# Matmuls of one fused kernel cut into 64-row halves, two heads' sums and two side sums open at a time

## The chip, the core and the metric

The kernel runs on one core of one Trainium2 chip. The metric is the device time of a run in microseconds (us). The engines are named as the profile names them: PE (TensorE matmul), PEld (its weight loads), DVE (VectorE), ACT (ScalarE), POOL (GpSimd) and SP (SyncE, which here issues most DMAs).

## The reference

Two independent computations share one kernel; their outputs are put side by side.

```python
# A: a long convolution (S4): a kernel of 2048 taps per channel, 576 channels, applied through an FFT
K = einsum("dn,dnl,dn->dl", Cc, exp(dt*A*l), dt*B).real;  y = irfft(rfft(u)*rfft(K))[:2048] + u*Dskip
# B: attention, 32 query heads of 18 columns, one key head and one value head; S = 2048, D = 576
q = (x @ wq) per head; k = x @ wk; v = x @ wv
p = softmax(q k^T * 18**-0.5);  out = concat_heads(p @ v) @ wo
```

## The kernel before

**Attention.** Queries are worked in four chunks of 512 (`c`), heads in groups of four (`g`, eight per chunk), keys in 16 blocks of 128 (`kb`). One *step* is one (c, g, kb): two *pairs* of heads (`j`), so there are 512 steps and 1024 pairs. For each pair, `scores` (L501) multiplies a key block by the two heads' queries in f16: the two heads' 55 rows lie at rows 0 and 64 of the array, so both matmuls, 64 rows by 128 columns, run at once into the two PSUM banks of one tile `s`. `exponentials` (L512) then makes a tile `P` of 128x1024 on ACT. `product` (L802) multiplies the four heads' `P` by the values in f32, four matmuls of 128 rows by 32 columns side by side, and sums over the 16 key blocks in one PSUM bank, `ops`, which DVE copies out (`gather`).

PSUM has eight banks: three tiles `s` of two banks (`NS = 3`), one bank for `ops`, one (`bank()`, tag `f`) for everything else. The loop in `main` goes in rounds of NS pairs: three scores one after the other, their three exponentials, then products and side work until the tiles `s` are expected to be free.

**Side work on PE**, all in f32 and in 128 rows by 32 columns: query projections `q` (`qproj`, L395) for later chunks, the output projection `op` (`outproj`, `outproj_part`), small bounds `up`, and the convolution's matmuls: its taps `kg` (`kgen`, L1236), its transforms `hu`, `lu`, `hk`, `lk` (`transform`) and `iy` (`back`). DVE does the convolution's elementwise work between them and empties each bank.

**What sets the order.** PE, DVE and ACT are ordered by hand: `main` records instructions in the order in which a planner's clocks (`K.t` for PE, `K.v` for DVE, `K.a` for ACT) say that they become ready. Side work comes from generators (streams) that yield after each piece: kind `"p"` for a piece on PE, `"v"` for one on DVE; a stream that holds the bank `f` goes on before any other may take it. `state["credit"]` rations how much side work goes into a round; `RATE` and `PACE` ration the convolution's DVE work per step. Every engine executes its instructions in the recorded order.

Of the kernel before, what the change touches and what calls it, by code (L numbers as in the profile page):

```python
# [9 lines left out]
F32 = mybir.dt.float32  # L10
# [32 lines left out]
NS = 3  # L43
# [3 lines left out]
RATE = 1.90  # L47
PACE = 1.83
# [5 lines left out]
DEFER = 0.5  # L54
NAUG = 5
# [20 lines left out]
class Clock:  # L76
# [6 lines left out]
    def __init__(self):  # L83
        self.t = self.v = self.a = 0.0
        self.work = 0.0
        self.last = ""
        self.s = [0.0] * NS
        self.fill = 0.0

    def pe(self, cost, *after):  # L90
        self.t = max(self.t, *after) + cost if after else self.t + cost
# [103 lines left out]

class Attention:
# [7 lines left out]
    def __init__(self, tc, ctx, aps, clock):  # L204
# [11 lines left out]
        self.ps_f = pool("ps_f", 1, space=PSUM)  # L216

# [3 lines left out]
    def bank(self, n, name):  # L221
        self.k.pe(0.0, self.k.fill)
        return self.ps_f.tile([P, CT], F32, tag="f", name=name)[:, :n]
# [9 lines left out]
    def setup(self, tp, conv):  # L233
# [24 lines left out]
        nc.gpsimd.memset(x0[64:, 4, :], 0.0)  # L258
        nc.gpsimd.memset(xr[64:, 4], 0.0)
# [27 lines left out]
        p1, small = (self.ps_s.tile([P, 2, CT], F32, tag="s", name=n)[:, 0, :] for n in ("first", "small"))  # L287
        p2 = self.bank(CT, "second")
        pv = self.ps_o.tile([P, CT], F32, tag="o", name="vps")

        def queries(ps, j, k):
            nc.tensor.matmul(ps[32 * j:32 * j + 32, :], self.wq[0][:, k, 32 * j:32 * j + 32], x0[:, k, :],
                             start=(k == 0), stop=(k == 4), tile_position=(0, 32 * j))

        def project(ps, j, i, c, k):
            nc.tensor.matmul(ps[32 * j:32 * j + 32, :], wkv[:, k, i:i + 32], xr[:, k, c - 1, :] if c else x0[:, k, :],
# [51 lines left out]
    def settle(self, conv):  # L348
# [4 lines left out]
        vp = self.bank(CT, "vp").rearrange("p (j n) -> p j n", j=4)  # L353
# [6 lines left out]
        pk = self.bank(20, "kmx")  # L360
# [4 lines left out]
        V.tensor_scalar(self.kmax, self.kmax, FLOOR, 1.002, op0=ALU.max, op1=ALU.mult)  # L365
        for m in range(2, 5):
# [9 lines left out]
    def load_wo(self):  # L376
        self.nc.vector.memset(self.wo[0:1, :, 0:1], 0.0)
        for m, (m0, mn) in enumerate(MT):
            self.nc.sync.dma_start(self.wo[:mn, m, :], self.a["wo"][m0:m0 + mn, :])

    def qproj(self, c, m, xt):

        nc, V, K = self.nc, self.V, self.k
        w, nf = self.wq[m], 2 if m < 4 else 1
        self.q_left = 5 * nf
        yield "p", K.fill, False
        ps = self.bank(CT, f"q{c}_{m}")
        for f in range(nf):
            for k in range(5):
                for j in range(4):  # L390

                    o = slice(32 * j, 32 * j + 32)
                    i = o if m < 4 else slice(32 * (j % 2), 32 * (j % 2) + 32)
                    x = slice(256 * f, 256 * f + 256) if m < 4 else slice(256 * (j // 2), 256 * (j // 2) + 256)
# [1157 lines left out]
```

## Time and profile before

| | us |
|---|---|
| runs (3) | 1164.48 to 1169.69, median 1167.79 |
| the profiled execution: its own time | 1169.43 |
| its span, first to last instruction | 1167.6 |
| PE busy / DVE busy / ACT busy / POOL busy | 1084.9 / 997.3 / 999.3 / 143.3 |
| mean granted TensorE clock | 0.99 |

The profile is one execution. In its rows a group of instructions has a count, its busy time, the mean duration of one in ns, and the idle time ahead of it with what ended it. Matmuls overlap in the array, so a matmul's recorded duration is longer than the distance between two of them; one f32 matmul leaves two records and one f16 matmul leaves one. In a timeline row stand the start, the length of the whole run of equal instructions, and their number.

### The profile page before, as it was taken

To read this page: it belongs to the slowest core of one execution; us is meant where nothing else is said; L and a number is where in the kernel's file an instruction comes from. 1 tells how busy PE (TensorE), PEld (TensorE's weight loads), DVE (VectorE), ACT (ScalarE), POOL (GpSimd) and SP (SyncE) were. 2 spreads that over 40 slices of the span, in tenths; PEclk is the share of its full clock that TensorE was granted. 3 is DMA by queue.
4 is the path that set the end of the run, shared out by engine and by line. 5 is a ranking of instruction groups with operands and counts; after the bars stand their busy time and mean duration, and the time that the engine had idled before them with its cause. 6 is when DMAs were issued, how large, how long until landed. Compare 5 with 4: busy or idle time off the path is not lost.

```text
span 1167.6 us, 33030 instructions
## 1 busy us (share of the span) xinstructions
PE 1084.9 (93%) x13862; PEld 391.0 (33%) x13862; DVE 997.3 (85%) x1741; ACT 999.3 (86%) x1052; POOL 143.3 (12%) x257
## 2 busy tenths in 40 slices
PE   6999899999999999889999999999889999998997
PEld 1333233333333333223333333334323333333233
DVE  3797997998996998998899797998898898897853
ACT  2888979898888988998888898888989988998993
POOL 5421320112022000001122000001220000000000
PEclk9899999999999999999999999999999999999999
DMA  7412242114113102112223202112212202112111
GB/s 224 141 41 75 75 140 79 49 41 136 37 61 104 53 29 86 36 65 85 85 83 97 85 20 71 50 55 79 72 40 76 87 29 74 59 48 69 35 42 44
DMA packets 58750, 83.35 MB, mean 71 GB/s; under 512 B 14467, under 2 KB 34679, under 8 KB 58085
## 3 DMA queue, kind: packets, MB, share of 16 engines
q1 hardware_dynamic: 47173, 73.39, 19.5%
q0 software_dynamic: 10848, 7.37, 2.5%
q8 instruction: 110, 1.80, 0.6%
q10 hardware_dynamic: 576, 0.43, 0.1%
q14 instruction: 43, 0.35, 0.1%
HBM read 46.59 MB, written 33.85 MB: 69 GB/s over the span
## 4 chain that ended last, share of the span: by engine, by line
PE 54%; DVE 25%; ACT 12%; issue 7%; DMA 2%; SPq 0%; ACTq 0%; DVEq 0%
PE ops L802 22%; PE s L501 14%; ACT P L512 11%; DVE tab L119 4%; PE op L193 4%; PE q L395 3%; PE iy L193 3%; PE kg L1236 3%; DVE acc L119 3%; DVE ks L119 3%; DVE pt L119 2%; DVE t L119 2%; DVE fr L119 1%; DMA xr<-xT 1%; PE hk L193 1%
## 5 line engine op out<-in xcount | busy, mean ns | idle before, releaser
L512 ACT ACTIVATE P<-s 128x1024 f32<-128x1024 f32 x992 | 934.8, 1034 | 123.1 <-PE s L501 121.6
L802 PE MATMUL ops<-P,v_sb 128*32 128x512 f32 x4096 | 513.4, 600 | 12.7 <-DVE o L123 12.4
L501 PE MATMUL s<-aug,kaug 55*128 55x512 f16 x2048 | 308.7, 383 | 40.0 <-ACT P L512 36.1
L501 PEld LDWEIGHTS <-kaug 55*128 55x128 f16 x2048 | 90.5, 94 | 374.3 <-issue 330.9
L802 PEld LDWEIGHTS ops<-P,v_sb 128*32 128x32 f32 x4096 | 116.2, 110 | 166.6 <-issue 124.1
L445 POOL DMA_DIRECT2D qd<-qh x116 | 65.8, 574 | 337.5 <-DVE qh L127 334.9
L395 PE MATMUL q<-x,wq_sb 128*32 128x256 f32 x1360 | 84.6, 385 | 3.4 <-DVE sck L119 2.5
L193 PE MATMUL op<-wo_sb,oT 126*32 126x288 f32 (+1 forms) x1104 | 79.6, 411 | 1.1 <-DVE ob L123 1.1
L119 DVE TENSOR_TENSOR tab<-tab,tt 128x576 f32<-128x576 f32 (+1 forms) x72 | 59.2, 823 | 1.6
L119 DVE TENSOR_TENSOR tt<-fr,sum 128x576 f32<-128x576 f32 (+1 forms) x72 | 58.9, 819 | 0.0
L119 DVE TENSOR_TENSOR tab<-tab 128x576 f32<-128x576 f32 (+1 forms) x72 | 58.9, 818 | 0.0
L119 DVE TENSOR_TENSOR tab<-sum,fr 128x576 f32<-128x576 f32 (+1 forms) x72 | 58.9, 818 | 0.0
L119 DVE TENSOR_TENSOR tab<-fr,dif 128x576 f32<-128x576 f32 (+1 forms) x72 | 58.8, 817 | 0.0
L123 DVE COPY ksb<-kg 128x192 f32<-128x192 f32 x48 | 17.4, 362 | 47.6 <-PE kg L1236 47.3
L395 PEld LDWEIGHTS q<-x,wq_sb 128*32 128x32 f32 x1360 | 40.1, 110 | 44.1 <-issue 18.1
L1145 POOL MEMSET fr<- 128x192 f32 x24 | 12.8, 618 | 301.8 <-DVE tt L119 176.3
L119 DVE TENSOR_TENSOR acc<-acc,pt 128x1728 f32<-128x1728 f32 (+2 forms) x36 | 48.7, 1352 | 0.1
L119 DVE TENSOR_TENSOR pt<-us,ks 128x1728 f32<-128x1728 f32 (+2 forms) x36 | 48.4, 1352 | 0.1
L510 ACT ACTIVATE P<-s,bias 128x1024 f32<-128x1024 f32 x32 | 33.2, 1114 | 15.1 <-PE s L501 14.7
L193 PEld LDWEIGHTS op<-wo_sb,oT 126*32 126x32 f32 (+1 forms) x1104 | 30.4, 109 | 42.1 <-issue 17.8
L1236 PE MATMUL kg<-tab 128*32 128x64 f32 x2304 | 41.9, 220 | 2.5 <-DVE tab L119 1.6
L1236 PEld LDWEIGHTS kg<-tab 128*32 128x32 f32 x2304 | 35.5, 110 | 25.2 <-issue 9.2
(157 smaller groups left out, 1023.2 us busy)
## 6 DMA issues: line engine op xcount, KB each, us to landing
od<-o SPq DMA_DIRECT2D x31, 256.0 KB
aug<-qd SPq DMA_DIRECT2D x124, 55.0 KB
u<-u SPq DMA_DIRECT2D x12, 384.0 KB
kd<-ksb SPq DMA_DIRECT2D x12, 384.0 KB
kt<-kd SPq DMA_DIRECT2D x48, 96.0 KB
outa<-u SPq DMA_DIRECT2D x12, 384.0 KB
pw<-pw SPq DMA_DIRECT2D x8, 528.0 KB
oT<-od SPq DMA_DIRECT2D x16, 252.0 KB
```

The lines of the kernel that those rows point to most:

```text
L119: return self.v.tensor_tensor(out, *a, **k)
L123: return self.v.tensor_copy(out, *a, **k)
L193: nc.tensor.matmul(ps[j:e], w[:, j:e], x, start=start, stop=stop, tile_position=(0, j))
L395: nc.tensor.matmul(ps[o, 256 * f:256 * f + 256], w[:, k, i], xt[:, k, x], start=(k == 0), stop=(k == 4), tile_position=(0, 32 * j))
L445: q.dma_start(qd[h:h + n, row + d:row + d + nd, cs], src[i1:i1 + n * nd, :cs.stop - cs.start])
L501: nc.tensor.matmul(ps[:, j, :], self.kaug[r, kb * P:(kb + 1) * P], t[r, :], start=True, stop=True)
L510: nc.scalar.activation(pt, ps, AF.Exp, bias=self.bias, scale=SCALE / QQ)
L512: nc.scalar.activation(pt, ps, AF.Exp, scale=SCALE / QQ)
L802: nc.tensor.matmul(o_ps[32 * j:32 * j + 32, :], self.v[:, kb, :], pts[2 * n + j // 2][:, j % 2, :], start=(kb == 0), stop=(kb == 15), tile ...
L1145: nc.gpsimd.memset(t[:, :, 0:NF:8], one)
L1236: nc.tensor.matmul(ps[32 * g:32 * g + 32, d, :], t[:, :32], t[:, 32:], start=(j == 0), stop=(j == 1), tile_position=(0, 32 * g))
```

## The change

All products of the loop take tiles of 64 rows by 32 columns instead of 128 by 32 (or, for scores, 64 by 128).

- **Two sums at a time.** A new class `Turns` gives `part`: eight matmuls, four on rows 0 to 63 that add to one bank (`y = role`) and four on rows 64 to 127 that add to the other. Then the halves change banks: a second `part` with the other role completes both sums. Its first matmul waits on a semaphore that the last matmul of the first part sets, since the halves swap the banks that they write.
- **Heads.** `schedule()` pairs the last eight key blocks of one group of heads with the first eight of the next; their two sums are the two banks of `ops` (`obank`). A step of four pairs makes two parts. The first eight and the last 24 key blocks stand alone and stay at 128 rows.
- **Side work.** `bank()` gives two banks. `q`, `op`, `up`, `hu`/`lu`/`hk`/`lk` (now one tile `fu`, `fk`) and `iy` are made in the two roles; `kg` stays at 128 rows. Rows 64 to 127 of the fifth tile of x and wq, of which only 64 were in use, now hold a copy of the first 64, so that `q` takes nine parts for its two halves of queries; the fifth tile of `oT` and `wo` is padded with zeros to 100 rows. One DVE copy empties both banks.
- **Scores** become eight matmuls for a pair, 55 rows by 32 columns.
- **PSUM**: two tiles `s` (`NS = 2`, four banks), two banks for `ops`, two for side work. The loop goes pair by pair: `work(i)` places products and side pieces until tile `s` is free, then come one pair's scores. `DUE` and `LIMIT_P` say how many pairs after its exponentials a part may, and must, be placed.
- The planner's numbers are new: 0.12 us when the rows change, `SWAP` 0.36 us between two parts, `RATE` 1.87, `PACE` 1.80, `DEFER` 0.35, `NAUG` 6.

```diff
-NS = 3
+NS = 2
-RATE = 1.90
-PACE = 1.83
+RATE = 1.87
+PACE = 1.80
-    def pe(self, cost, *after):
+    def pe(self, cost, *after, rows=64):
+        if rows != self.rows:
+            self.t += 0.12
+            self.rows = rows
...
+class Turns:
+    def part(self, nc, role, outs, ws, xs, rows=((0, 64), (64, 128)), start=False, stop=False, first=False, last=False, only=None):
+        m = None
+        for r in (0, 1):
+            lo, hi = rows[r]
+            y = r ^ role
+            if hi <= lo or only is not None and y != only:
+                continue
+            for j in range(4):
+                w, x = ws(y, j), xs(y, j)
+                q = nc.tensor.matmul(outs(y, j), w[lo:hi], x[lo:hi], start=start if start in (0, 1) else start[y], stop=stop if stop in (0, 1) else stop[y], tile_position=(64 * r, 32 * j))
+                if m is None and first:
+                    q.wait_op(self.sem, self.n, "sem-ge")
+                m = q
+        if last:
+            self.n += 1
+            m.then_inc(self.sem, 1)
...
     def scores(self, i, c, pr, kb, cost):
-            nc.tensor.matmul(ps[:, j, :], self.kaug[r, kb * P:(kb + 1) * P], t[r, :], start=True, stop=True)
+            for b in range(0, P, 32):
+                nc.tensor.matmul(ps[b:b + 32, j, :], self.kaug[r, kb * P + b:kb * P + b + 32], t[r, :], start=True, stop=True, tile_position=(64 * j, b))
...
-        def product(n):
-            for j in range(4):
-                nc.tensor.matmul(o_ps[32 * j:32 * j + 32, :], self.v[:, kb, :], pts[2 * n + j // 2][:, j % 2, :],
-                                 start=(kb == 0), stop=(kb == 15), tile_position=(0, 32 * j))
+        def product():
+            if len(st) == 2:
+                q = self.to.part(nc, state["role"], lambda y, j: o_ps[y][32 * j:32 * j + 32, :], lambda y, j: self.v[:, at[y][1], :],
+                                 lambda y, j: pts[at[y][0] + j // 2][:, j % 2, :], start=[ph == 0 and at[y][1] == 0 for y in (0, 1)],
+                                 stop=[ph == 1 and at[y][1] == 15 for y in (0, 1)], first=(ph == 1), last=(ph == 0))
+                state["swap"] = K.t + SWAP
...
-        for r in range(0, len(pairs), NS):
-            new = range(r, min(r + NS, len(pairs)))
-            for i in new:
-                ss[i] = self.scores(i, c, 2 * g + j, kb, 0.34 if i == r else 0.216)
+        for i, (c, g, kb, j, n, y) in enumerate(pairs):
+            if i > 2:
+                work(i)
+            ss = self.scores(i, c, 2 * g + j, kb, 0.216)
...
+def schedule():
+    group = lambda n, kb: (n // 8, n % 8, kb, n % 2)
+    steps = [[group(0, kb)] for kb in range(8)]
+    for t in range(8, 8 * (8 * NCH - 1)):
+        n = t // 8
+        steps.append(sorted((group(n, t % 8), group(n - 1, 8 + t % 8)), key=lambda x: x[3]))
+    steps += [[group(8 * NCH - 2, kb)] for kb in range(8, 16)]
+    steps += [[group(8 * NCH - 1, kb)] for kb in range(16)]
```

Where the change moves PE's instructions, two places show it. The first is the loop in the middle of the run, on PE: `s` are scores (the two numbers in a name are the head pair within the chunk and the key block), `ops` are products (the number is the group of heads), `kaug` is a weight load for scores. Before, there are three scores, then products at 128 rows.

```order
L802 MATMUL ops_5_6292<-P_10_9_6429,v_sb 32x512 x2
L802 MATMUL ops_5_6292<-P_11_9_6449,v_sb 32x512 x2
L802 MATMUL ops_5_6292<-P_10_10_6451,v_sb 32x512 x2
L802 MATMUL ops_5_6292<-P_11_10_6453,v_sb 32x512 x2
L501 LDWEIGHTS kaug
L501 MATMUL s_11_12_6493<-aug_112,kaug 128x512 [waits Activation_49]
L501 MATMUL s_10_13_6496<-aug_111,kaug 128x512 [waits Activation_49]
L501 MATMUL s_11_13_6499<-aug_112,kaug 128x512 [waits Activation_49]
L802 MATMUL ops_5_6292<-P_10_11_6474,v_sb 32x512 x2
```

After, on PE in the same part of the loop, one part of a product stands between two pairs' scores, half of it for each of two groups; the second part, with the banks exchanged, comes two pairs later and waits for the semaphore `o`.

```order
L218 MATMUL ops_1_7158<-P_2_9_7986,v_sb 32x512 x2
L218 MATMUL ops_1_7158<-P_3_9_8044,v_sb 32x512 x2
L218 MATMUL ops_2_8025<-P_4_1_7953,v_sb 32x512 x2
L218 MATMUL ops_2_8025<-P_5_1_7964,v_sb 32x512 x2
L565 LDWEIGHTS kaug
L565 MATMUL s_2_10_8100<-aug_110,kaug 32x512 [waits Activation_49]
L565 MATMUL s_3_10_8119<-aug_111,kaug 32x512 [waits Activation_49]
L218 MATMUL ops_2_8025<-P_4_1_7953,v_sb 32x512 [waits o]
L218 MATMUL ops_2_8025<-P_5_1_7964,v_sb 32x512 x2
L218 MATMUL ops_1_7158<-P_2_9_7986,v_sb 32x512 x2
L565 MATMUL s_4_3_8138<-aug_112,kaug 32x512 [waits Activation_49]
```

So the order on PE goes from threes of scores with 128-row work between to single pairs of scores with one 64-row piece between.

The second place is the convolution's last transform, `iy`, on PE, with scores (`s`) and products (`ops`) around it. Before, its 16 matmuls for one bank stand together.

```order
L501 MATMUL s_13_3_6646<-aug_114,kaug 128x512
L193 MATMUL iy_6655<-w_6457,dft_sb 32x192 [waits DVE_49]
L193 MATMUL iy_6655<-w_6457,dft_sb 32x192 x15
L802 MATMUL ops_6_6682<-P_12_0_6572,v_sb 32x512 [waits DVE_49]
L802 MATMUL ops_6_6682<-P_12_0_6572,v_sb 32x512
```

After, on PE, the sixteen matmuls of the first role come in two pieces with a pair's scores between them, and those of the second role follow later, behind the semaphore `f`.

```order
L218 MATMUL iy_8066<-w_7560,dft_sb 32x192 [waits DVE_49]
L218 MATMUL iy_8066<-w_7560,dft_sb 32x192 x7
L565 MATMUL s_5_2_8081<-aug_113,kaug 32x512
L218 MATMUL iy_8066<-w_7560,dft_sb 32x192 x8
L218 MATMUL iy_8066<-w_7560,dft_sb 32x192 [waits f]
L218 MATMUL iy_8066<-w_7560,dft_sb 32x192 x15
```

Thirty-two matmuls now fill two banks that DVE empties with one addition, where sixteen filled one. Over the whole of PE's order, up to the end of the loop and its tail, neighbouring matmuls differ in rows (64 against 128) at 684 places before and at 152 places after; 240 matmuls of products wait for `o` and 130 of side work for `f`.

438 lines of the change are left out of this document (256 added, 182 removed).

## The prediction

> **What bounds the kernel now.** I read the page's busy times first, then the costliest groups, the busy times by stage, the waits, and last one stretch of the timeline.
>
> ```profile
> span 1167.6 us, 33030 instructions
> PE 1084.9 (93%) x13862; PEld 391.0 (33%) x13862; DVE 997.3 (85%) x1741; ACT 999.3 (86%) x1052; POOL 143.3 (12%) x257
> PE 54%; DVE 25%; ACT 12%; issue 7%; DMA 2%; SPq 0%; ACTq 0%; DVEq 0%
> L512 ACT ACTIVATE P<-s 128x1024 f32<-128x1024 f32 x992 | 934.8, 1034 | 123.1 <-PE s L501 121.6
> L802 PE MATMUL ops<-P,v_sb 128*32 128x512 f32 x4096 | 513.4, 600 | 12.7 <-DVE o L123 12.4
> L501 PE MATMUL s<-aug,kaug 55*128 55x512 f16 x2048 | 308.7, 383 | 40.0 <-ACT P L512 36.1 <-ACT P L510 1.0 <-DMA qd<-keys 0.9
> L510 ACT ACTIVATE P<-s,bias 128x1024 f32<-128x1024 f32 x32 | 33.2, 1114 | 15.1 <-PE s L501 14.7
> ```
>
> PE is the fullest and leads the chain that ended last (third line: shares by engine). ACT idles 121.6 us waiting for PE's scores, PE 36.1 us waiting for ACT and 12.4 us for DVE to empty `ops`: PE is late most of the time, and at other times stands still.
>
> By stage (columns: stretch, length, then busy time and instructions of PE, PEld, DVE, ACT, POOL; clock; DMA):
>
> ```profile
> 0.00:27.00 27.00, 16.44 (x132) 4.23 (x132) 8.28 (x21) 6.60 (x8) 13.11 (x28) 1.00 0.79 237
> 27.00:60.00 33.00, 30.86 (x297) 11.44 (x297) 23.21 (x67) 27.75 (x27) 14.08 (x25) 0.84 0.46 131
> 200.00:1000.00 800.00, 755.67 (x9884) 274.86 (x9880) 722.52 (x1255) 708.42 (x748) 85.04 (x151) 1.00 0.21 67
> 1100.00:1147.50 47.50, 45.08 (x464) 14.37 (x465) 27.31 (x43) 43.23 (x47) 0.00 (x0) 1.00 0.09 30
> 1147.50:1167.60 20.10, 13.80 (x192) 6.30 (x186) 8.51 (x16) 0.79 (x3) 0.00 (x0) 0.93 0.17 62
> ```
>
> The exponentials run from about 27.0 to 1147.5, so the loop takes 1120.5 us, 2.19 us for each of 512 steps; 47.1 us lie outside it. DVE has 997.3 - 8.3 - 8.5 = 980.5 us of work in the loop, 1.92 us a step; in the long middle it is busy 722.5 of 800, 0.903.
>
> What a round costs shows in the timeline (start, length of the run, count):
>
> ```profile
> 237.90 1.04 PE L802 MATMUL ops<-P,v_sb 128*32 128x512 f32 x8
> 238.87 0.82 PE L501 MATMUL s<-aug,kaug 55*128 55x512 f16 x6
> 239.36 2.86 ACT L512 ACTIVATE P<-s 128x1024 f32<-128x1024 f32 x3 [0.62 <-PE s L501]
> 239.62 1.50 PE L395 MATMUL q<-x,wq_sb 128*32 128x256 f32 x24
> 240.94 1.04 PE L802 MATMUL ops<-P,v_sb 128*32 128x512 f32 x8
> 508.06 1.90 PE L802 MATMUL ops<-P,v_sb 128*32 128x512 f32 x16
> 499.67 6.65 ACT L512 ACTIVATE P<-s 128x1024 f32<-128x1024 f32 x7
> 500.79 0.39 PE L501 MATMUL s<-aug,kaug 55*128 55x512 f16 x2 [0.53 <-ACT P L512]
> ```
>
> A product leaves eight records that run four at a time; two products of sixteen records last 1.90, so one set of four follows the next after (1.90 - 0.60)/3 = 0.433 and a product takes 0.866. Six scores (three pairs) last 0.82 and one 0.39, so a pair takes (0.82 - 0.39)/2 = 0.215. But from product to scores pass 238.87 - 237.90 = 0.97, 0.10 more than the product, and from three pairs to `q` 239.62 - 238.87 = 0.75, 0.105 more than three pairs. From `q` to product, both at 128 rows, nothing like it stands: 1.32 for six sets, 0.22 each. So a change of rows costs about 0.105 us on each side. An exponential follows another after (2.86 - 1.03)/2 = 0.915; ACT's need is 2 x 0.915 a step, and 999.3 - 934.8 - 33.2 = 31.3 us of other work, 0.06 a step: 1.89 in all. ACT alone could do the loop in 968 us, DVE in 980.
>
> **What goes.** Row changes fall from 684 to 152 by PE's order; kg and the products that stand alone keep theirs. 532 x 0.105 = **-56 us** on PE, which is late in most rounds, so I take all of it.
>
> The second and third score of a round wait with PE idle for their tiles, since leaving the scores costs two changes. Pair by pair, PE fills that time with pieces. Of the 36.1 us (range 0 to 36) I take **-20**; nearer the upper end, because the cause goes, but not all, because two tiles also make PE wait.
>
> With two banks for `ops`, DVE empties one while PE sums in the other: 12.4 us, range 0 to 12, **-10**.
>
> **What stays equal.** A part is eight matmuls at half the rows: two parts finish two steps, so if eight small matmuls run beside each other as four do now, 0.866 a step remains. Scores run on both row halves at once into two banks already (six records in 0.82), so two halves with two banks exist in this trace, though for sums in f32 they don't. A pair now has eight matmuls and eight loads for its 0.215. The nearest rows for many short ones:
>
> ```profile
> L1236 PE MATMUL kg<-tab 128*32 128x64 f32 x2304 | 41.9, 220 | 2.5 <-DVE tab L119 1.6
> L1236 PEld LDWEIGHTS kg<-tab 128*32 128x32 f32 x2304 | 35.5, 110 | 25.2 <-issue 9.2
> L501 PEld LDWEIGHTS <-kaug 55*128 55x128 f16 x2048 | 90.5, 94 | 374.3 <-issue 330.9
> ```
>
> 2304 matmuls with as many loads in 41.9 us: 0.018 us for each; eight need 0.15, less than 0.215. Their loads, 2304 x 0.110 = 253 us one after another, hide in those 41.9 us. So I charge the scores nothing; bounds are 0 and, if four loads of a row half each stood in front of the pair at a quarter of the 94 ns for 128 columns, 0.094 x 1024 = 96 us. I take 0, by the kg rows. The Trainium skill ("TensorE: Matmul & The Clock Gate", Part 3: Packing small matmuls) says that a weight load overlaps running matmuls only where its row group differs. This trace disagrees: kg's loads and matmuls all span the same 128 rows. By the rule the sum would be 96 us higher, 1198; by the row, 1102.
>
> **What comes.** 370 matmuls wait for the part before theirs. The latest they can be late is the pipeline's tail, 0.600 - 0.433 = 0.17, if nothing lies between: 0 to 63 us. In the order shown with the change, scores and other pieces lie between; where a stream has nothing else it stands. I take one in six, **+10**.
>
> Two tiles `s` instead of three narrow the coupling. PE's score starts 500.79 - 499.67 = 1.12 after the exponential whose tile it takes over; the next exponential starts 239.36 - 238.87 = 0.49 after it. With two tiles this must fit in 2 x 0.915 = 1.83: 0.22 to spare, where three tiles left 1.13. A product part and a pair take 0.866 + 0.215 = 1.08, 0.17 over the 0.915 between two exponentials: it just fits. A part with a side piece of 0.44 (two sets of `q`) in the same gap doesn't: ACT waits 0.17 + 0.44 - 0.22 = 0.39. I take 0.02 a step (one step in twenty), **+10**, range 0 to 60.
>
> Nothing for these: the zeroing of `oT` is a POOL instruction ahead of SP's load of `oT`, and on POOL it queues behind stores that wait for DVE:
>
> ```profile
> POOL qd L445 <- DVE qh L127: 334.9, 19, 85.1
> DVE ksb L123 <- PE kg L1236: 36.9, 24, 3.0
> ```
>
> But there are three such zeroings, well ahead of use, and SP's next query tiles behind them are one tile further ahead (six for five). If that cover fails, a few us each. The extra load into rows 64 to 127 of x0 passes on SP before weights not used until later. Fewer, longer DVE copies save a few tenths in all. The first part of the loop (clock 0.84) is as before.
>
> **Sum.** On the profiled execution's 1169.4: -56 - 20 - 10 + 10 + 10 = -66, so 1103.4. It lay 1.6 above the median of the runs (1167.8): **1102**. The loop would be 1054 us, 2.06 a step, above ACT's 1.89. DVE must then do 980.5 us in 1054, 0.93. In the middle its 722.5 us, spread a little later by `RATE` (1.87 for 1.90: 711), would stand in 800 x 1054/1120.5 = 752: 0.945 against 0.903 now. The last 47.5 us of the loop, with 27.3 of DVE work, can take what is moved. That is tight, and gives the first rival.
>
> **Rivals.**
>
> *DVE becomes the bound.* If its waits for PE (36.9 us at kg alone in the middle) keep it at 0.903, the loop needs 33 + (980.5 - 23.2)/0.903 = 1093, with 47 outside **1140**. For: PE, ACT and DVE needs lie close together. Against: those waits are for a late PE, and PE becomes less late. Up to 1155 if its share falls to 0.89. Chance 0.23.
>
> *Two tiles starve ACT: slower.* If the recorded order puts a part and a side piece into one gap in every step, ACT waits 0.39 a step: 1.89 + 0.39 = 2.28, times 512, and 47: **1214**. From 0.30 a step on (2.19 - 1.89) it is slower than before. For: slack 0.22 against 1.13, pieces of 0.44 and 0.87. Against: the planner fills gaps only up to the time when the tile is free plus 0.35. Chance 0.07.
>
> *Row halves one after another: slower.* If the lower half starts only with the upper half's second set, it lags 0.433, and scores after a part find half the array taken: 512 x 0.433 = 222, **1324**. It decides from 0.13 us a step. The Trainium skill, same page and part, says that matmuls start and end strictly in program order; a part that lists upper tiles first, with two sets each, would lag so. Against: eight records in 1.04 us show four tiles beside each other in a set although each has two sets. Chance 0.06.
>
> *Loads exposed*, as priced: **1198**; decides from 0.064 us a pair. Chance 0.04.
>
> *The pairing gives back what it saves*: all 370 waits exposed, 63, and 0.04 a step of ACT's waiting, 20: 1169.4 - 86 + 83 - 1.6, **1165**. Chance 0.03.
>
> **How the numbers follow.** The forecast has 0.57, from 1064 (-56 - 36 - 12, nothing added: 1169.4 - 104 - 1.6) to about 1130; DVE's case reaches 1155. 1064 to 1155 leaves out the 0.20 of the last four. About 0.5% is what a measurement of this kernel can tell from no change. Faster: 0.57 + 0.23 = 0.80; same 0.03; slower 0.17.
>
> **What would show it.** Right: in the timeline, scores after a part begin 0.87 to 0.88 after it; `ops` has eight records in a set and keeps 0.43 between sets; PE's wait for DVE's `o` is gone; ACT's wait for `s` falls from 121.6 us to some 60; DVE in the middle at 0.93 or more. The first rival shows as DVE's share unmoved and more PE waits for DVE; the second as ACT's wait for `s` grown, in short pieces after products; the third as sets of four records; the fourth as more than 0.215 from pair to pair. A time over 1162 makes the prediction wrong.

## The result and the profile after

The changed kernel takes 1197.29 us (median of four runs, 1193.83 to 1198.27) against 1168.32 for the kernel before (four runs): 1.0251 times as long, 95% interval 1.0225 to 1.0277. It is 29 us slower. The profiled execution took 1198.27 us, with a span of 1196.4 and a mean clock of 0.982.

The first view cuts both executions at the same four points of the work: the exponentials of pair 0, pair 64 and pair 960, and the end of the last one. Columns: the stretch, its length, then busy time and instructions of PE, PEld, DVE, ACT and POOL, the granted clock, the DMA share and GB/s. Before:

```profile
27.10:100.80 73.70, 71.06 (x910) 27.18 (x914) 55.95 (x119) 63.65 (x66) 24.60 (x44) 0.93 0.32 92
100.80:1082.30 981.50, 921.48 (x11986) 333.13 (x11978) 884.44 (x1525) 868.13 (x915) 105.54 (x186) 0.99 0.22 68
1082.30:1147.40 65.10, 61.96 (x654) 20.22 (x652) 39.93 (x64) 59.99 (x64) 0.00 (x0) 1.00 0.10 32
1147.40:1167.60 20.20, 13.90 (x196) 6.30 (x186) 8.61 (x16) 0.89 (x3) 0.00 (x0) 0.93 0.17 62
```

After:

```profile
27.40:116.90 89.50, 74.45 (x1936) 36.14 (x1933) 60.75 (x128) 64.49 (x66) 32.90 (x59) 0.90 0.33 98
116.90:1092.70 975.80, 894.64 (x25344) 465.59 (x25344) 863.90 (x1469) 877.42 (x915) 98.01 (x175) 0.99 0.21 67
1092.70:1159.60 66.90, 64.86 (x1473) 25.07 (x1459) 48.55 (x73) 61.09 (x65) 0.00 (x0) 1.00 0.14 49
1159.60:1196.40 36.80, 24.03 (x364) 10.60 (x360) 18.89 (x32) 0.93 (x3) 0.00 (x0) 0.83 0.12 45
```

The loss has two places. The first 64 pairs take 89.5 us instead of 73.7 (+15.8), and what follows the last exponential takes 36.8 instead of 20.2 (+16.6). The 896 pairs between, where the forecast had nearly all of its gain, take 975.8 instead of 981.5 (-5.7); the last 64 pairs +1.8. With 0.3 of lead-in that makes the 28.8 us by which the spans differ. In the middle PE is busy 0.917 instead of 0.939, DVE 0.885 instead of 0.901: neither came closer to its limit.

The costliest groups after (count | busy us, mean ns | idle before and its releasers), and the long middle:

```profile
L576 ACT ACTIVATE P<-s 128x1024 f32<-128x1024 f32 x992 | 946.2, 1034 | 114.6 <-PE s L565 105.5 <-ACT P L576 0.2
L218 PE MATMUL ops<-P,v_sb 64*32 64x512 f32 x7680 | 525.0, 594 | 3.6 <-issue 2.6 <-DVE o L127 0.7
L565 PE MATMUL s<-aug,kaug 55*32 55x512 f16 x8192 | 426.2, 383 | 65.6 <-ACT P L576 53.7 <-issue 2.7 <-ACT P L574 2.6
L565 PEld LDWEIGHTS <-kaug 55*32 55x32 f16 x8192 | 178.3, 90 | 360.5 <-issue 325.6 <-DMA aug<-qd 1.4 <-DMA db<-rden 0.3
...
200.00:1000.00 800.00, 736.34 (x20983) 384.26 (x20991) 711.10 (x1212) 718.12 (x750) 85.68 (x154) 0.99 0.22 68
```

PE's wait for DVE's `o` is gone (0.7 us, 12.4 before). ACT's wait for scores fell only from 121.6 to 105.5, and PE's wait for an exponential to free its tile grew from 36.1 to 53.7.

A piece of the middle in the timeline (start, length of the run, count, idle before it):

```profile
602.05 0.41 PE L565 MATMUL s<-aug,kaug 55*32 55x512 f16 x8 [0.50 <-ACT P L576]
...
602.26 1.05 PE L218 MATMUL ops<-P,v_sb 64*32 64x512 f32 x16
...
603.12 0.41 PE L565 MATMUL s<-aug,kaug 55*32 55x512 f16 x8
...
603.34 0.85 PE L218 MATMUL fk<-kt,dft_sb 64*32 64x192 f32 x32
...
603.99 0.41 PE L565 MATMUL s<-aug,kaug 55*32 55x512 f16 x8
...
604.21 1.05 PE L218 MATMUL ops<-P,v_sb 64*32 64x512 f32 x16
```

The parts work as they were meant to. Sixteen records in 1.05 us are two sets of eight, so eight tiles run side by side. From part to score pass 603.12 - 602.26 = 0.86 and from score to part 0.22: the 0.1 us on each side of a score are gone. The first row shows what stands instead: PE, half a microsecond idle, waits for a tile.

Where the start loses, ACT waits 8.75 us for the scores of pair 11, which stand behind the second group's queries and bounds on PE:

```profile
42.43 4.48 PE L218 MATMUL q<-x,wq_sb 64*32 64x256 f32 x144 [0.33 <-DVE un L139]
...
49.49 0.69 PE L218 MATMUL up<-sel_sb,aw 64*32 64x4 f32 x30 [2.58 <-DVE aw L131]
...
50.34 1.26 SPq L553 DMA_DIRECT2D aug<-qd  x3
...
51.57 2.12 ACT L574 ACTIVATE P<-s,bias 128x1024 f32<-128x1024 f32 x2 [8.75 <-PE s L565]
```

`schedule()` lets group 1 begin at step 8, which is pair 16, and the loop demands a group's queries eight pairs ahead. Before, it began at pair 32. In the same stretch ACT stands still a second time, 5.61 us at 108.57, behind a stop of PE of 4.96 us that no semaphore ended (its rows are in the last section).

And where the end loses, the last chunk of the convolution isn't done when the loop ends; its DVE work, two transforms back and only then the last head group's division come one after the other:

```profile
1163.08 1.83 DVE L123 TENSOR_TENSOR acc<-acc 128x768 f32<-128x768 f32 x2
1164.93 1.97 DVE L123 TENSOR_TENSOR sv<-acc 128x384 f32<-128x384 f32 x4
1166.82 1.96 DVE L123 TENSOR_TENSOR w<-sv 128x384 f32<-128x384 f32 x4
...
1167.51 3.97 PE L218 MATMUL iy<-w,dft_sb 64*32 64x192 f32 x64 [6.00 <-DVE w L123]
...
1172.20 3.19 PE L218 MATMUL iy<-w,dft_sb 64*32 64x192 f32 x64 [0.71 <-DVE u L123]
...
1176.51 0.38 ACT L709 ACTIVATE o_last<-ops 128x256 f32<-128x256 f32 x1 [16.76 <-DVE rc_last L708]
```

### The profile page after: what moved, and what is told of

Its sections match the earlier page's. It is cut to its first block, busy times and chain, and to the rows that moved or that the text cites. A ratio compares the mean times of both kernels' runs of the same rounds, so it can differ in the third digit from the quotient of the medians.

```text
span 1196.4 us, 63338 instructions
## 1 busy us (share of the span) xinstructions
PE 1075.6 (90%) x29238; PEld 541.8 (45%) x29238; DVE 1000.3 (84%) x1718; ACT 1010.5 (84%) x1052; POOL 142.2 (12%) x259
## 4 chain that ended last, share of the span: by engine, by line
PE 52%; ACT 30%; DVE 10%; issue 7%; DMA 1%; ACTq 0%; POOL 0%; DVEq 0%
ACT P L576 28%; PE ops L218 16%; PE s L565 12%; PE op L218 5%; PE q L218 5%; PE kg L1353 3%; PE ops L893 2%; PE iy L218 2%; PE fu L218 2%; PE fk L218 2%; DVE tab L123 1%; PE fin L197 1%; DMA aug<-keys 1%; ACT P L574 1%; DVE acc L123 1%
## 5 line engine op out<-in xcount | busy, mean ns | idle before, releaser
L576 ACT ACTIVATE P<-s 128x1024 f32<-128x1024 f32 x992 | 946.2, 1034 | 114.6 <-PE s L565 105.5
L218 PE MATMUL ops<-P,v_sb 64*32 64x512 f32 x7680 | 525.0, 594 | 3.6 <-issue 2.6
L565 PE MATMUL s<-aug,kaug 55*32 55x512 f16 x8192 | 426.2, 383 | 65.6 <-ACT P L576 53.7
L565 PEld LDWEIGHTS <-kaug 55*32 55x32 f16 x8192 | 178.3, 90 | 360.5 <-issue 325.6
L218 PEld LDWEIGHTS ops<-P,v_sb 64*32 64x32 f32 x7680 | 150.2, 106 | 41.8 <-issue 7.3
L218 PE MATMUL q<-x,wq_sb 64*32 64x256 f32 (+1 forms) x2736 | 84.8, 355 | 2.5 <-issue 1.7
L218 PE MATMUL op<-wo_sb,oT 64*32 64x288 f32 (+2 forms) x2144 | 84.4, 410 | 1.9 <-DVE sck L123 1.9
L218 PEld LDWEIGHTS q<-x,wq_sb 64*32 64x32 f32 x2736 | 52.3, 106 | 28.1 <-issue 8.4
L123 DVE TENSOR_TENSOR tt<-fr,sum 128x576 f32<-128x576 f32 (+1 forms) x72 | 58.9, 818 | 0.0
L218 PEld LDWEIGHTS op<-wo_sb,oT 64*32 64x32 f32 (+2 forms) x2144 | 40.6, 108 | 34.5 <-issue 17.1
L218 PE MATMUL iy<-w,dft_sb 64*32 64x192 f32 x1536 | 47.0, 339 | 7.4 <-DVE w L123 6.0
L218 PE MATMUL fu<-u,dft_sb 64*32 64x192 f32 x1536 | 49.6, 330 | 2.1 <-DVE scu L123 2.0
```

The lines of the kernel that those rows point to most:

```text
L123: return self.v.tensor_tensor(out, *a, **k)
L218: q = nc.tensor.matmul(outs(y, j), w[lo:hi], x[lo:hi], start=start if start in (0, 1) else start[y], stop=stop if stop in (0, 1) else stop ...
L565: nc.tensor.matmul(ps[b:b + 32, j, :], self.kaug[r, kb * P + b:kb * P + b + 32], t[r, :], start=True, stop=True, tile_position=(64 * j, b))
L576: nc.scalar.activation(pt, ps, AF.Exp, scale=SCALE / QQ)
```

## The experiments

All ratios are to the kernel before, run on the same chip; differences between two changed versions are differences of their ratios times 1167 us. The table gives the four stretches of each profiled execution, worked out from its trace as above; kernels that leave out part of the work have a star. In e2, e4, e17 and e18 the order of instructions is that of their base; in all others the planner made a new order, and such an order can by itself move the time by 1 to 2% (e10 to e13).

| | pairs 0-63 | 64-959 | 960-1023 | after the loop | median us | ratio (95%) |
|---|---|---|---|---|---|---|
| before | 73.7 | 981.5 | 65.1 | 20.2 | 1168.32 | 1 |
| after | 89.5 | 975.8 | 66.9 | 36.8 | 1197.29 | 1.0251 (1.0225 to 1.0277) |
| e1 | 78.9 | 974.6 | 67.0 | 35.8 | 1183.65 | 1.0129 (1.0100 to 1.0157) |
| e2 | 89.1 | 1052.2 | 71.6 | 36.5 | 1277.86 | 1.0939 (1.0920 to 1.0957) |
| e3 | 83.6 | 1011.8 | 70.6 | 41.7 | 1236.40 | 1.0574 (1.0549 to 1.0599) |
| e4 | 72.9 | 984.2 | 65.8 | 20.5 | 1173.07 | 1.0047 (1.0029 to 1.0065) |
| e5* | 70.0 | 955.0 | 63.5 | 22.5 | 1139.65 | 0.9779 (0.9750 to 0.9807) |
| e6* | 88.7 | 946.8 | 66.7 | 75.3 | 1209.24 | 1.0379 (1.0331 to 1.0427) |
| e7* | 81.4 | 968.5 | 69.2 | 20.2 | 1168.15 | 1.0015 (0.9993 to 1.0037) |
| e8* | 72.9 | 990.7 | 63.0 | 17.4 | 1171.71 | 1.0049 (1.0026 to 1.0072) |
| e9 | 77.6 | 1031.8 | 70.3 | 17.5 | 1225.45 | 1.0501 (1.0482 to 1.0520) |
| e10 | 76.9 | 981.3 | 68.9 | 20.3 | 1181.53 | 1.0132 (1.0110 to 1.0154) |
| e11 | 81.2 | 988.7 | 70.7 | 20.1 | 1191.70 | 1.0210 (1.0182 to 1.0238) |
| e12 | 74.9 | 970.2 | 69.2 | 21.6 | 1164.41 | 0.9990 (0.9971 to 1.0009) |
| e13 | 76.5 | 978.2 | 70.4 | 18.3 | 1174.40 | 1.0065 (1.0045 to 1.0085) |
| e14* | 75.3 | 964.4 | 69.9 | 22.5 | 1161.78 | 0.9954 (0.9938 to 0.9970) |
| e15* | 75.2 | 987.7 | 67.0 | 23.9 | 1183.49 | 1.0137 (1.0097 to 1.0178) |
| e16 | 71.8 | 993.1 | 63.8 | 27.8 | 1183.44 | 1.0132 (1.0101 to 1.0163) |
| e17* | 72.9 | 955.6 | 68.8 | 21.9 | 1148.02 | 0.9856 (0.9824 to 0.9888) |
| e18* | 70.0 | 961.9 | 64.9 | 20.0 | 1147.15 | 0.9849 (0.9817 to 0.9881) |

**e1: the pairing begins later.**

```diff
-    steps = [[group(0, kb)] for kb in range(8)]
-    for t in range(8, 8 * (8 * NCH - 1)):
+    steps = [[group(0, kb)] for kb in range(16)] + [[group(1, kb)] for kb in range(8)]
+    for t in range(16, 8 * (8 * NCH - 1)):
```

> The changed kernel with one edit: group 0 (16 steps) and the first 8 steps of group 1 run alone, and two groups share a step only from then on, so that the second group's queries are wanted at pair 32 as in the kernel before and not at pair 16. Theory 'early queries': ACT's idle 8.75 us ahead of pair 11 goes, and some 10 to 16 us of the 28.8 that the change cost come back: 1181 to 1187, ratio 1.011 to 1.017. Rival 'the queries only stand elsewhere' (PE has the same work to do in the first 64 pairs, and pays it a little later): 1195 to 1199, ratio 1.023 to 1.027.

Measured: 14 us faster than the changed kernel, in the range of the first theory; in the traces 10.6 of these lie in the first 64 pairs. ACT's 8.75 us are gone: its longest wait in the 40 us after the first exponential is now 2.90. So the early demand for queries is shown as a cause, worth some 6 us by ACT's waits. The rest isn't shown to be its doing: the stop of PE behind ACT's second wait of 5.61 isn't in e1's trace either, and the edit does nothing that was meant to remove it. In e3 and e7 the demand is as early (ACT waits 8.1 us there) and no such stop stands in the first 64 pairs; these take 83.6 and 81.4 us, between e1 and the changed kernel.

**e2, e4: the form of the scores, undone in the changed kernel and done alone in the kernel before.**

```diff
-            for b in range(0, P, 32):
-                nc.tensor.matmul(ps[b:b + 32, j, :], self.kaug[r, kb * P + b:kb * P + b + 32], t[r, :], start=True, stop=True, tile_position=(64 * j, b))
+            nc.tensor.matmul(ps[:, j, :], self.kaug[r, kb * P:(kb + 1) * P], t[r, :], start=True, stop=True)
```

(e4 is the same edit backwards, on the kernel before.)

> The changed kernel with one edit undone: a pair's scores are again two matmuls of 55x128 instead of eight of 55x32; nothing else differs, the order of all other work is word for word the same. Theory 'short scores' (eight matmuls finish later: 0.540 us from the first of them to the exponential against 0.491, and they double PE's instruction fetches, whose stops took some 16 us against 4): in the middle ACT waits 0.05 less in each of the 360 pairs in which it waits, 18 us, and up to half of the extra 12 us of stops goes: 1173 to 1187, ratio 1.004 to 1.017. Rival 'the form costs nothing': 1195 to 1199. Rival 'a change of columns costs as a change of rows does' (scores of 128 columns between parts of 32): slower than the changed kernel, by up to 0.2 us for each of some 800 visits, 1200 to 1350.

> The kernel before with one part of the change alone: a pair's scores are eight matmuls of 55x32 instead of two of 55x128; three tiles, rounds of three, all products on 128 rows. Theory 'short scores': the later end of the scores (0.05 us) is paid once a round and the doubled instruction fetches stop PE for some 10 us more: 342 x 0.05 = 17 and up to 10, so 1185 to 1196, ratio 1.014 to 1.023. Rival 'the form costs nothing': 1166 to 1171, ratio 0.998 to 1.002. The prediction's bound for exposed loads would be 96 us more.

Measured: e4 costs 5.5 us, less than the theory of short scores said, and far from 96. e2 is 80 us slower than the changed kernel: the third theory. PE in the timeline of e2:

```profile
640.56 1.09 PE L218 MATMUL ops<-P,v_sb 64*32 64x512 f32 x16
641.59 0.39 PE L564 MATMUL s<-aug,kaug 55*128 55x512 f16 x2
641.92 1.09 PE L218 MATMUL ops<-P,v_sb 64*32 64x512 f32 x16
642.94 0.39 PE L564 MATMUL s<-aug,kaug 55*128 55x512 f16 x2
```

From part to score now pass 1.03 instead of 0.86, from score to part 0.33 instead of 0.22, although both use 64 rows. A change from 32 to 128 columns costs what a change of rows costs, or a little more. PE comes to scores 744 times in this trace; at 0.28 us a visit that is an estimate of some 208 us of PE's time, of which 80 show, a share of about 0.4. The Trainium skill ("TensorEngine Tiling (Array Packing)", section Key Properties) says that changing the tiling mode drains TensorE, while another tile of the same mode doesn't; the 0.17 and 0.11 of e2, and the 0.86 and 0.22 of the changed kernel without them, agree. The small scores, which the prediction took as a risk, are what makes the change work at all.

**e3: the products back on 128 rows, all else as changed.**

```diff
-                q = self.to.part(nc, state["role"], ...)
-                K.pe(0.857, done[e + 3] + 0.1, state["swap"] if ph else 0.0)
+                for j in range(4):
+                    nc.tensor.matmul(o_ps[y][32 * j:32 * j + 32, :], self.v[:, at[y][1], :], pts[p + j // 2][:, j % 2, :],
+                                     start=(at[y][1] == 0), stop=(at[y][1] == 15), tile_position=(0, 32 * j))
+                K.pe(0.857, done[p + 1] + 0.1, rows=128)
```

> The changed kernel with the products of the loop undone: where two groups share a step, their two products run one after the other on all 128 rows instead of in 64-row halves; the two tiles of scores, the two banks, the pairing of groups and all side work stay in the new form. PE then changes rows 1067 times instead of 152, which is 96 us of its time at 0.105 each. Theory 'PE's time is what the loop waits for' (the prediction's): 60 to 96 us slower than the changed kernel, 1257 to 1293, ratio 1.076 to 1.107. Rival 'PE has idle time that takes it' (0.43 us a step in the middle, against 0.19 that the changes cost): 1197 to 1225, ratio 1.025 to 1.049.

Measured: 38 us slower than the changed kernel for 96 us more on PE, a share of 0.39. Neither theory's range is met: PE's idle time takes more than half, but not all.

**e5, e6, e14: less work for PE, in the kernel before, the changed one, and e12.**

```diff
+            w = CT if kb in (0, 15) else 440
-                nc.tensor.matmul(o_ps[32 * j:32 * j + 32, :], self.v[:, kb, :], pts[2 * n + j // 2][:, j % 2, :],
+                nc.tensor.matmul(o_ps[32 * j:32 * j + 32, :w], self.v[:, kb, :], pts[2 * n + j // 2][:, j % 2, :w],
-            K.pe(0.88, done[...
+            K.pe(0.88 * w / CT, done[...
```

(e5; e6 and e14 likewise, 432 columns.)

> The kernel before with less PE work and nothing else: the products of key blocks 1 to 14 of each group run on 440 of their 512 columns (the output is then incomplete). That takes 512 x 14/16 x 0.866 x 72/512 = 54.6 us from PE, as much as the 56 us of row changes that the prediction took off the path. Theory 'PE's time is what the loop waits for': 54 us faster, 1113, ratio 0.953. Rival 'part of PE's time lies under other waits' (in e3 96 us more of PE's time cost 39, a share of 0.41): 22 us faster, 1145, ratio 0.981. Rival 'ACT and DVE set the loop': 1160 to 1168, ratio 0.995 to 1.

> The changed kernel with the same kind of edit: 432 of 512 columns in the products of all shared steps in which neither group has key block 0 or 15 (output incomplete): 360 parts x 0.866 x 80/512 = 48.7 us off PE. Theory 'PE's time is what the loop waits for': 49 us faster than the changed kernel, 1148, ratio 0.983. Rival 'PE has idle time of 0.43 us a step' with the share 0.41 of e3: 20 us faster, 1177, ratio 1.008. Rival 'two tiles: ACT and PE wait for each other whatever PE's need is': 1190 to 1197, ratio 1.019 to 1.025.

> e12 with 48.7 us of PE's time left out as in e6 (products of shared steps on 432 of 512 columns where no group has key block 0 or 15; output incomplete). Theory 'PE's time is what the loop waits for': 49 us below e12's 1164: 1115, ratio 0.957. Share 0.4 to 0.5 as in the kernel before (e5) and in e3: 20 to 24 us, 1140 to 1145, ratio 0.979 to 0.983. Theory 'two tiles or DVE set the loop': 1155 to 1166, ratio 0.991 to 1.

Measured: in the kernel before, 54.6 us of PE's time are worth 26, a share of 0.47; the order is a new one, so part of this can be the order's doing. In the changed kernel 48.7 us shorten the loop by 30 us, but the time grows by 15, since 38 us more stand behind the loop: the planner packs the loop tighter and DVE's work doesn't follow, so this is outside all three ranges. In e12, where the end is clean, they are worth 4, in the range of its third theory. First e12's scores in its list of groups, then e14's exponentials and scores:

```profile
L565 PE MATMUL s<-aug,kaug 55*32 55x512 f16 x8192 | 423.3, 382 | 58.0 <-ACT P L576 48.0 <-ACT P L574 1.6 <-issue 1.1
```

```profile
L576 ACT ACTIVATE P<-s 128x1024 f32<-128x1024 f32 x992 | 938.1, 1041 | 107.6 <-PE s L565 102.7 <-ACT P L576 0.2
...
L565 PE MATMUL s<-aug,kaug 55*32 55x512 f16 x8192 | 441.6, 383 | 75.5 <-ACT P L576 68.9 <-ACT P L574 1.9 <-issue 1.5
```

PE's wait for a tile is 68.9 us against 48.0: 21 of the 49 us that PE saves it then waits for ACT.

**e7, e8, e15: less work for DVE, in the changed kernel, the kernel before, and e12.**

```diff
-            tt(im, im, re, op=ALU.add)
-            yield "v", 0.0, False
             tt(re, re, t, op=ALU.subtract)
```

> The changed kernel with less DVE work: the 72 additions of the tables' real part to the imaginary one are left out (the convolution's output is then another), 58.9 us of DVE's time (36.1 and 22.8). Theory 'DVE sets the middle' (the prediction's first rival): 45 to 59 us faster than the changed kernel, 1138 to 1152, ratio 0.975 to 0.987. Theory 'the convolution's rest after the loop': the loop stays, but its last part moves into the loop, and the 16.6 us that the end grew by go: 1179 to 1184, ratio 1.010 to 1.014. Rival 'DVE matters nowhere': 1195 to 1199.

> The kernel before with the same additions left out, 58.9 us of DVE's time. If DVE's time is part of what its loop waits for (0.903 busy in the middle), 20 to 59 us faster: 1108 to 1147, ratio 0.950 to 0.983. If PE's is (the prediction's view): 1160 to 1168, ratio 0.994 to 1.

> e12 with 58.9 us of DVE's time left out as in e7 and e8. Theory 'DVE sets the middle': 40 to 59 us below e12: 1105 to 1125, ratio 0.948 to 0.965. Theory 'DVE only made the end longer', which e12 has mended: 1155 to 1166, ratio 0.991 to 1.

Measured: the changed kernel gains 28 us of 58.9, and 16.6 of these are its end, which is back at 20.2: DVE's work set the end there. The time lies between the ranges of the two theories, since the middle and the start gave some too. The kernel before gains nothing (+6), and e12 loses 17; both are slower than either of their theories allowed. But these runs test the middle less than they seem to: with less work to place, the planner sets DVE's other work earlier, and in the traces DVE's busy time between pairs 64 and 960 falls by only 24 us in e8 (884.4 to 860.4), 22 in e15 (881.0 to 859.3) and 34 in e7 (863.9 to 830.3). So some 20 us less of DVE's work in the middle of e8 and e15 didn't shorten it. That DVE isn't a limit there isn't shown: e15 also has another order, and the orders of e10 to e13, with the same work, differ by as much (970 to 989 us in the middle).

**e9: two tiles in the kernel before** (`NS = 2`).

> The kernel before with one part of the change alone: two tiles for scores and rounds of two exponentials (NS = 2; the third tile of the last sums takes its two banks elsewhere). PE then changes rows 1024 times instead of 684: 340 x 0.105 = 36 us more of its time. Theory 'two tiles cost nothing by themselves': only those changes, at the share of 0.41 to 0.48 at which e3 and e5 count PE's time: 15 to 17 us, 1182 to 1184, ratio 1.013 to 1.015. Theory 'two tiles make ACT and PE wait for each other' (0.22 us of slack instead of 1.13): 30 to 70 us beside them, 1213 to 1253, ratio 1.039 to 1.074. The prediction's 0.02 us a step would be 10 us beside the changes' 36: 1213, ratio 1.039.

Measured: 58 us slower, in the range of the second theory. 340 more row changes, 36 us of PE's time, explain 14 to 17 at the shares of e3 and e5; some 42 are, by this estimate, the price of two tiles in rounds of two. Its groups:

```profile
L513 ACT ACTIVATE P<-s 128x1024 f32<-128x1024 f32 x992 | 951.2, 1023 | 163.7 <-PE s L502 158.9 <-ACT P L513 0.3
...
L502 PE MATMUL s<-aug,kaug 55*128 55x512 f16 x2048 | 355.1, 383 | 55.2 <-ACT P L513 42.2 <-ACT P L511 1.7 <-DMA qd<-keys 0.7
```

ACT waits 158.9 us for scores instead of 121.6, and PE 42.2 for ACT instead of 36.1. The changed kernel can't be run with three tiles, since its eight banks are full; so its own price for two is not measured.

**e10 to e13, e16: other numbers for the planner**, on e1 (e16: on the kernel before).

```diff
 e12:
-RATE = 1.87
-PACE = 1.80
+RATE = 1.97
+PACE = 1.9
-        return ps, K.t + 0.27
+        return ps, K.t + 0.36
-        K.s[i % NS] = K.act(0.925, max(ready, free)) + 0.1
+        K.s[i % NS] = K.act(0.95, max(ready, free)) + 0.1
```

> e1 with numbers of the planner changed so that it sets the convolution's last instructions inside the loop: 0.97 us instead of 0.925 for an exponential, RATE 1.95 and PACE 1.88. Theory 'the convolution's rest after the loop': the end falls from 35.8 us (e1) to 20 or 21 and the loop stays at 1115 to 1125, so 1162 to 1172, ratio 0.995 to 1.004, no slower than the kernel before. Rival 'DVE sets the loop': the loop takes up what the end loses, 1180 to 1187, ratio 1.010 to 1.017.

> e1 with other numbers of the planner to the same end: PE's side pieces are let in earlier (SPARE 0.3 instead of 0.8, the value of the kernel before; DEFER 0.5; RATE 1.97, PACE 1.90). Theory 'the convolution's rest': as e10, 1160 to 1172, ratio 0.993 to 1.004. Rival 'two tiles': each earlier piece meets a score or an exponential, ACT's waits grow, 1180 to 1195, ratio 1.010 to 1.024.

> e1 with the planner's scores 0.09 us later (0.36 instead of 0.27) and exponentials of 0.95, RATE 1.97 and PACE 1.90: the order leaves PE room for its late scores. If the order's being too tight is what makes PE and ACT wait in turn, the loop falls below e1's 1120.5 to 1095 to 1110 and the end to 21: 1143 to 1160, ratio 0.979 to 0.994, faster than the kernel before. If only the end shrinks: 1165 to 1172, ratio 0.998 to 1.004. If neither: 1180 to 1187.

> e12 with the planner's scores 0.45 us late instead of 0.36 (exponentials 0.95, RATE 1.97, PACE 1.90 as there). If tightness is still what the loop loses by, it gains again: loop 1095 to 1110, 1145 to 1160, ratio 0.982 to 0.995. If e12 is already loose enough, planned gaps are now paid: 1165 to 1180, ratio 0.999 to 1.012.

> The kernel before with the planner's numbers moved as in e12: scores 0.36 instead of 0.27, exponentials 0.95 instead of 0.925, RATE 2.00, PACE 1.93. Theory 'two tiles need a looser order, three don't': 1166 to 1185, ratio 1.000 to 1.016. Theory 'any order of this planner is too tight': as much faster as e12 against e1 (1.4%): 1150, ratio 0.986.

Measured: all four on e1 bring the end from 35.8 to 18 to 22 us, as expected. What the loop makes of it differs: in e10 and e11 it grows by 7 and 20 us, in e12 it falls by 6, in e13 it grows by 5. So e10 and e11 came out as their rivals said, not as the theory that only the end was wrong, and e13 as a loose order whose gaps are paid. e12 is as fast as the kernel before, not faster as its first theory had it (the loop takes 1114 us, not 1095 to 1110):

```profile
27.20:102.10 74.90, 70.73 (x1621) 27.58 (x1624) 57.38 (x117) 65.26 (x65) 25.12 (x45) 0.95 0.31 93
102.10:1072.30 970.20, 895.65 (x25606) 467.89 (x25592) 881.04 (x1503) 879.23 (x914) 107.43 (x188) 0.99 0.23 70
1072.30:1141.50 69.20, 66.69 (x1564) 26.34 (x1560) 43.30 (x64) 61.22 (x65) 0.00 (x0) 1.00 0.15 47
1141.50:1163.10 21.60, 15.62 (x228) 7.26 (x220) 8.99 (x16) 0.90 (x3) 0.00 (x0) 0.98 0.16 58
```

Start and end are back (74.9 and 21.6), DVE has 0.908 in the middle, and the middle is 11 us shorter than before, the last 64 pairs 4 longer. How much of the 11 us is the change and how much a lucky order isn't shown: e10 and e13 leave the middle 0 and 3 us shorter than before, e11 makes it 7 longer. The same loosening makes the kernel before 1.3% slower (e16), so it is no free gain of any order.

**e17, e18: shorter scores, in e12 and in the kernel before, orders unchanged.**

```diff
-        t = self.aug[16 * c + pr]
+        t, w = self.aug[16 * c + pr], CT if i < 8 else 256
...
-                nc.tensor.matmul(ps[b:b + 32, j, :], ..., t[r, :], ...)
+                nc.tensor.matmul(ps[b:b + 32, j, :w], ..., t[r, :w], ...)
...
+            ps = ps[:, :, :256].unsqueeze(2).broadcast_to([P, 2, 2, 256])
```

> e12, its order unchanged, with scores from pair 8 on only on 256 of their 512 columns; each exponential reads these columns twice, so that its own work stays 1024 elements a row (the output is then another). That takes 0.107 us off every pair's scores, 109 us of PE's time, and it shortens the way from a freed tile to the next exponential by the same 0.107: with two tiles 1.83 - 1.12 - 0.43 = 0.28 to 0.33 us of slack instead of 0.22. Theory 'the link over two tiles holds the loop': 40 to 90 us below e12's 1164, so 1074 to 1124, ratio 0.921 to 0.964, far more than e14's 3 us for 49 of products. Theory 'ACT and DVE are the bound': 1150 to 1164, ratio 0.986 to 0.999. If the edit slows the exponential, its mean says so.

> The kernel before, its order unchanged, with the same edit (scores on 256 columns from pair 9 on, exponentials of the same size; output another): 109 us less of PE's time with three tiles. At the share of 0.48 that e5 gave: 52 us faster, 1114, ratio 0.955. If ACT's need or DVE stops it sooner: 1125 to 1150, ratio 0.965 to 0.986.

Measured: 109 us less on PE, and less than a fifth of it comes back: 16 us in e12, 18 in the kernel before. That is the fast edge of "ACT and DVE are the bound" in e17, and the slow edge of its counterpart in e18. The exponentials aren't slower for it: back to back they start 0.90 us apart in both, 0.90 to 0.91 in their bases. The link over two tiles, shortened by 0.107, brings no 40 us, and two tiles and three end at nearly the same time, 1148 and 1147. e17's groups:

```profile
L579 ACT ACTIVATE P<-s 128x1024 f32<-128x1024 f32 x992 | 939.0, 1053 | 95.4 <-PE s L565 90.0 <-ACT P L579 0.5
...
L565 PE MATMUL s<-aug,kaug 55*32 55x256 f16 (+1 forms) x8192 | 335.8, 277 | 90.5 <-ACT P L579 79.7 <-issue 2.8 <-ACT P L577 2.3
```

ACT still waits 90.0 us for PE (92.4 in e12) and PE 79.7 for ACT (48.0 in e12), each in turn. One thing more stands in these traces. With PE far below its old share, the middle of e17 and that of e18 have, together with e5's, the highest shares of DVE of all runs. First e17's middle, then e18's:

```profile
98.30:1054.00 955.70, 832.26 (x25608) 457.08 (x25595) 879.46 (x1503) 871.12 (x915) 106.55 (x188) 0.99 0.23 71
```

```profile
96.40:1058.30 961.90, 850.67 (x11986) 335.74 (x11978) 882.69 (x1526) 863.50 (x915) 105.11 (x186) 0.99 0.22 69
```

DVE is busy 0.920 and 0.918 of them, and 0.919 in e5, against 0.901 before.

## Why the prediction was wrong

- **Row changes, -56: the size on PE was right, the worth was not.** They are gone in the timeline (0.86 and 0.22). The step that failed is "PE, which is late in most rounds, so I take all of it". In the kernel before, 54.6 us of PE's time are worth 26 (e5), 109 are worth 18 (e18); 96 put back into the changed kernel cost 38 (e3). So the share of PE's time that counts is 0.39 to 0.47 for 55 to 96 us (e5, e3) and falls to 0.17 for 109 (e18); at the first two the 56 us would be worth 22 to 26. The middle stands at 955.0, 955.6 and 961.9 in three runs with much less work on PE (e5, e17, e18), and in the kernel before at 981.5: in these runs PE's time gave some 26 us there at most, not 86. Only e6 went below (946.8), with 38 us more behind the loop. In the changed kernel the middle fell by 5.7. The prediction named ACT's 968 and DVE's 980 us as the next limits of the loop, as if each could run without waiting for the others.
- **-20 for PE's waits inside rounds: wrong sign.** PE's wait for ACT grew by 17.6 us.
- **-10 for the second bank: right in the profile** (12.4 to 0.7). What it is worth by itself no run shows.
- **+10 for the waits between parts: small.** The list of waits shows PE's loads waiting for the part before in some 60 cases, 20.6 us in all; PE itself stands idle for such a wait only some 2 us. The two largest of the loads' waits are these:

```profile
PEld q L218 <- PE q L218: 6.5, 16, 0.6
...
PEld ops L218 <- PE ops L218: 4.3, 16, 1.0
```

- **+10 for two tiles: too small in the kernel before** (some 42 us, e9, in rounds of two). In the changed kernel an estimate can be had from e3, which has 1067 row changes and all else in the new form. Its middle is 30.3 us longer than that of the kernel before; 383 more row changes explain 16 to 19 at the shares of e3 and e5, which leaves 11 to 15 for two tiles and the rest of the new form together. The order's own 1 to 2% is as large, so the size isn't shown.
- **"The first part of the loop is as before": wrong by 15.8 us.** The prediction read `schedule()` for its banks, not for when the second group's queries come due; and it had no term for a stop of PE that no semaphore ends.
- **"The last 47.5 us can take what is moved": wrong by 16.6 us.** DVE's work in the last stretch did rise (48.6 against 39.9 us in the last 64 pairs), but a chain of convolution steps was left, each waiting for the one before; e7, with less DVE work, and e10 to e13, with other numbers for the planner, bring the end back to 18 to 22.
- **Scores as eight matmuls at nothing: nearly right** (5.5 us, e4), and so the fourth rival is out. The Trainium skill's rule there ("TensorE: Matmul & The Clock Gate", Part 3), as the prediction quotes it, doesn't hold in these traces: 8192 loads of 90 ns, four for each row half of a pair, cost 5.5 us in all where the prediction's bound for it was 96. The same part makes an exception for a load into the background weight buffer; whether that is at work no run here shows.
- **DVE as the bound (0.23): wrong for this kernel, open for a faster one.** DVE's share didn't rise, it fell to 0.885, though its unfinished work is the 16.6 us after the loop. But this rival's loop of 1093 us is near where the loop ends up when PE's work is cut: it takes 1089 us in e5, 1097 in e17 and in e18, with DVE at 0.92 in the middle.
- **Two tiles starve ACT (0.07):** slower, as it said, but not by its mechanism: ACT's wait for scores fell by 16 us.
- **The pairing gives back what it saves (0.03):** its place was right, the middle, and its reason wrong: not the waits between parts, but the small worth of what was saved.
- **Row halves one after another (0.06): out.** The sets have eight records, and scores follow a part after 0.86. The Trainium skill's rule that matmuls start and end in program order (same page and part as above) isn't contradicted by it, as far as the records tell: eight records start within 0.04 us of each other, the other eight 0.43 later, and starts and ends go up together. What failed is the step from the rule to a lag of one half.

What stays open is what holds the middle near 955 us when PE has up to 109 us less to do. The waits name ACT and PE in turn, and neither less PE time (e14) nor a shorter link (e17) moves it far. DVE, busy 0.92 there, is the nearest rival and stands untested: e15 cut its work from e12, not from a kernel that stood at 955, and in another order. To settle it, DVE's work would have to be cut from e17 or e18 with their order kept; which chain it is was not found.

## What to carry to other kernels

Before you book PE time as a gain, take away the same time by another edit and see what it is worth: here half of 55 us, with a new order (e5), and a sixth of 109, with the order kept (e18). In a kernel whose order is planned, look at what a change in the loop's structure does to the due times of work at its start and to what is left at its end; here start and end lost 32 us, more than the 26 that the middle gave in e5. And a new order by itself moves such a kernel by 1 to 2% (e10 to e13), so a single edit is best tried with the order held fixed.

## What the runs showed of the hardware

- A change of the tile's columns, 32 to 128, costs PE 0.17 us going in and 0.11 coming back, at the same rows (e2).
- Eight f32 matmuls of 64 rows by 32 columns into two banks run side by side, each with its two records; sets stand 0.43 us apart, as sets of four with 128 rows do.
- Twice the instructions on PE bring twice the traffic of the queue that loads instructions. Before, then after (packets, MB, share):

```profile
q8 instruction: 110, 1.80, 0.6%
...
q8 instruction: 230, 3.77, 1.3%
```

PE also stops now and then where no semaphore ended the wait, the longest time here:

```profile
101.69 0.86 PE L1353 MATMUL kg<-tab 128*32 128x64 f32 x42
107.50 0.44 PE L1353 MATMUL kg<-tab 128*32 128x64 f32 x6 [4.96 <-issue]
```

Nine such stops of over 0.5 us stand in the trace of the changed kernel, 12.8 us in all, and none in that of the kernel before. Each of the nine ends 0.9 to 1.5 us after a packet of queue 8 has ended. Over all 20 traces it is 63 of 64 stops, 0.7 to 1.6 us after such a packet; in the changed kernel these stretches make up only 18% of the span, so chance would not put them there. The kernels with 182 packets or more have all such stops; those with 110, and e4 with 158, have none. So late instructions, which reach PE after it could have started them, are the likely cause. No run changed them alone, and what the stops cost in time isn't shown. The expectation of e2 reckons with 16 us of stops after and 4 before; the list of waits gives 15.5 for all of them, short ones too, after and none before.
